# Sliding-window attention block on one core: score sets of five chunks cut into 32x64 tiles, 50 sets for 60

## The chip, the cores and the metric

The kernel runs on one core of one Trainium2 chip. The metric is device time in microseconds (us) of one launch; less is better. A core has five engines with an instruction queue each: PE (TensorE, matrix products; PEld are its weight loads), ACT (ScalarE), DVE (VectorE), POOL (GpSimd) and SP (here only DMA issues).

## The reference, cut to what matters

x has 2048 rows of 640. The block is a modulated LayerNorm, windowed attention with 32 heads of 20, a gated sum, a second LayerNorm and a gated MLP (1536 wide):

```python
qkv = (x @ wqkv).reshape(B, S, 3, 32, 20)          # h of LayerNorm 1 stands for x
scores = einsum('bhqd,bhkd->bhqk', q, k) * 20 ** -0.5
mask = (idx[:, None] - idx[None, :] >= 0) & (idx[:, None] - idx[None, :] < 256)
p = softmax(where(mask, scores, -1e9))
x = x + ga * (einsum('bhqk,bhkd->bhqd', p, v) @ wo)
x = x + gb * ((sigmoid(h2 @ w_gate) * (h2 @ w_up)) @ w_down)   # h2: LayerNorm 2 of x
```

A query sees itself and the 255 positions before it.

## The kernel before

The 2048 rows are eight chunks (0 to 7) of 256 queries, two blocks of 128 each. For a chunk and four key blocks (two blocks back, one back, and the chunk's own two: -2, -1, 0, 1) the heads go in two groups q of 16; a group is four k, and each k is four heads j that stand in the four 32-row strips of PE (20 of the 32 rows are used).

- **Scores.** One score set fills the single buffer S, four PSUM banks (bank j for strip j) of 512 columns: keys lie on the 128 partitions, queries along the columns. A matmul for strip j is `tp=(32*j, 0)`, a 32x128 tile: four heads at a time. From chunk 1 on a group has six sets: for each k one with key blocks 0 and -1 against both query blocks (8 matmuls of 256 columns), and for each pair of k one with the two edge products, block -2 against query block 0 and block 1 against query block 1 (16 matmuls of 128).
- **Exp and masks.** ACT takes exp of the whole set (128x2048) into one of eight buffers E; no maximum is taken off. POOL then sets the dead part of the triangular blocks to zero with affine_select (L983 and L985): 512 elements each per partition in the main sets, 1024 in the edge sets.
- **Weighted sum.** `burst` is the product with V for a group: 64 matmuls of 256 or 128 columns in 128x32 tiles, `tp=(0, 32*j)`, four heads at a time in four column strips. It waits for all masks of its group. With `AFTER = 1` it stands ahead of the second score set of the next group, in the same planned step (`both_of`).
- **The rest of PE's work**: q, k, v projections, output projection (wo), MLP (wg, wu, wd), all in full 128x128 tiles and recorded on L625; tiled matmuls are L626.
- **Order.** Every operation has a place in a hand-out table: `PLAN` is a list of numbers (operation times 5 plus engine) that a planner made offline, and `SLOTS` the buffer that each tile takes. Each engine issues in that order and waits by semaphore.
- **Q and K transposed.** From chunk 1 on, DMA transposes on SP's queue turn the staged q and k into QT and KT (QT is [block, head group, query]).

Of the kernel before, what the change touches and what calls it, by code (L numbers as in the profile page):

```python
# [305 lines left out]
def c_pe(n):  # L306
# [119 lines left out]
PQ = ()  # L426
KEEP = 3
DSAFE = 1.0
NPB = 0
OUTE = ("sp", "act")  # L430
XE = ("sp", "act")
MW = 64
WM1 = (3, 5)
QM = ()
AFTER = 1
NOW = 1
LEAD = 2
HEAT = (5, 1, 1, 1)
# [8 lines left out]
def build(nc, A_x, A_wqkv, A_wo, B_x, B_w_gate, B_w_up, B_w_down, c, w_mod, out, S=2048):  # L447
# [480 lines left out]

    last = {"s": heat}

    def plan(a):


        if a == 0:
# [115 lines left out]
    def attention(a):  # L1050
# [8 lines left out]
        for q in range(2):  # L1059
            sets = plan(a)  # L1060
            Es = []
            for si, (ps, md, mf) in enumerate(sets):
                now = pend.pop(0) if pend and si == AFTER else None
                Es.append(score_set(a, q, si, ps, md, mf, now[0]() if now else None))
                if now:
                    now[1]()
# [175 lines left out]
```

## Time and profile before

| | |
|---|---|
| time of 3 runs | median 329.04 us (327.99 to 329.66) |
| profiled execution, first to last instruction (span) | 327.1 us |
| median less that span | 1.9 us |
| PE busy | 318.7 us, 97% |
| ACT busy | 231.4 us, 71% |
| DVE busy | 196.7 us, 60% |
| POOL busy | 183.0 us, 56% |
| granted TensorE clock | 1.000 |

The profile is of one execution; of its time only the span is recorded. Busy time of PE counts overlapping matmul records once. In lists of groups each row is a line, an engine, an operation and its tiles, with the count behind x, the busy time and the mean length of one record in ns, and then the idle time just ahead of them with what ended it. A matmul record lasts from its start to its modelled end, so records overlap; what a matmul takes of PE is the distance to the next start. In the timeline, rows are start, length, engine, line, operation, tiles, count.

### The profile page before, as it was taken

The page shows a single profiled execution, that of the slowest core. Times are in us where ns is not written, and L with a number is a line of the kernel's source. Part 1 is how long each engine was busy: PE and PEld are TensorE (multiplying, and loading weights), DVE is VectorE, ACT ScalarE, POOL GpSimd, SP SyncE. Part 2 cuts the span into 40 slices and gives each one's busy share as a digit, 9 for nine tenths or more (in the row PEclk, how much of TensorE's full clock was granted, in tenths as well). Part 3 has the DMA queues.
Part 4 walks back from the last instruction along what each step waited for, and adds up shares of the span by engine and source line. Part 5 has one row for each costly group of instructions (what it writes and reads, how often), then busy time and mean ns, then how long its engine had stood idle before and what let it go on. Part 6 is the DMA issues. An engine that isn't in the chain of part 4 may idle for free.

```text
span 327.1 us, 9812 instructions
## 1 busy us (share of the span) xinstructions
PE 318.7 (97%) x4123; PEld 227.8 (70%) x4123; DVE 196.7 (60%) x422; ACT 231.4 (71%) x227; POOL 183.0 (56%) x279
## 2 busy tenths in 40 slices
PE   5999899999999999999999999999999999999997
PEld 2666556567776777665767667766777777788885
DVE  6796799678485545675457554456727463484333
ACT  2489799987787898879797968785897568322120
POOL 4248579789688563778383745646490837402000
DMA  7989899999902281321802100360051012202101
GB/s 231 373 319 196 178 271 192 222 289 274 218 18 40 42 139 34 82 42 44 170 0 44 32 2 19 80 125 2 1 82 42 2 42 43 82 0 42 40 2 40
DMA packets 64613, 33.52 MB, mean 102 GB/s; under 512 B 49082, under 2 KB 63034, under 8 KB 64570
## 3 DMA queue, kind: packets, MB, share of 16 engines
q1 hardware_dynamic: 63200, 31.27, 42.2%
q10 hardware_dynamic: 1370, 1.64, 1.5%
q8 instruction: 32, 0.52, 0.7%
q14 instruction: 11, 0.09, 0.1%
HBM read 18.35 MB, written 2.62 MB: 64 GB/s over the span
## 4 chain that ended last, share of the span: by engine, by line
PE 93%; DMA 3%; DVE 1%; ACT 1%; issue 0%; POOL 0%; SPq 0%; DVEq 0%
PE M L625 77%; PE S L626 9%; PE M L626 7%; DMA QT<-stg 1%; DMA x<-in_A_x_dram 1%; ACT E L975 1%; DVE st L732 1%; DVE x L753 0%; SPq L524 0%; POOL st L740 0%; ACT QT L655 0%; DVE hT L814 0%; DVE st L734 0%; DVE x L1159 0%; POOL st L738 0%
## 5 line engine op out<-in xcount | busy, mean ns | idle before, releaser
L975 ACT ACTIVATE E<-S 128x2048 bf16<-128x2048 f32 x90 | 169.0, 1877 | 36.3 <-PE S L626 34.4
L983 POOL TENSOR_SCALAR_AFFINE_SELECT E<-E 128x512 bf16<-128x512 bf16 (+2 forms) x90 | 73.7, 830 | 36.2 <-ACT E L975 15.1
L985 POOL TENSOR_SCALAR_AFFINE_SELECT E<-E 128x512 bf16<-128x512 bf16 (+1 forms) x84 | 65.6, 790 | 36.4 <-ACT E L975 30.7
L625 PE MATMUL M<-h2T,wu 128*128 128x256 bf16 x480 | 73.6, 273 | 0.0
L625 PE MATMUL M<-h2T,wg 128*128 128x256 bf16 x480 | 72.7, 273 | 0.0
L1140 DVE SCALAR_TENSOR_TENSOR hh<-sig,M 128x512 bf16<-128x512 f32 x48 | 32.4, 681 | 49.5 <-ACT sig L1138 27.2
L625 PE MATMUL M<-wd,hh 128*128 128x320 bf16 (+2 forms) x396 | 60.5, 295 | 0.0
L625 PEld LDWEIGHTS M<-h2T,wu 128*128 128x128 bf16 x480 | 45.1, 98 | 10.8 <-issue 2.7
L1138 ACT ACTIVATE sig<-M 128x512 f32<-128x512 f32 x48 | 28.5, 596 | 33.5 <-PE M L625 32.4
L625 PEld LDWEIGHTS M<-h2T,wg 128*128 128x128 bf16 x480 | 45.2, 98 | 9.9 <-issue 1.9
L625 PEld LDWEIGHTS M<-wd,hh 128*128 128x128 bf16 x396 | 36.8, 98 | 14.9 <-issue 1.9
L626 PE MATMUL S<-QT,KT 20*128 20x256 bf16 (+1 forms) x960 | 35.9, 245 | 1.8 <-DMA QT<-stg 1.3
L626 PEld LDWEIGHTS S<-QT,KT 20*128 20x128 bf16 x960 | 14.1, 92 | 21.9 <-ACT E L975 11.6
L732 DVE BATCH_NORM_STATS2 st<-x 128x6 f32<-128x320 bf16 x64 | 29.0, 476 | 0.6 <-DMA x<-in_A_x_dram 0.5
L625 PE MATMUL M<-wk,hT 128*128 128x320 bf16 x160 | 29.4, 300 | 0.0
L1021 DVE STREAM_TRANSPOSE T<-M 128x512 f32<-128x512 f32 x32 | 21.6, 698 | 12.7 <-PE S L626 12.2
L625 PE MATMUL M<-wv,hT 128*128 128x320 bf16 x160 | 28.6, 300 | 0.0
L625 PE MATMUL M<-wo,oT 128*128 128x320 bf16 x160 | 28.0, 300 | 0.0
L625 PE MATMUL M<-wq,hT 128*128 128x320 bf16 x160 | 27.6, 300 | 0.3 <-DVE hT L814 0.3
L1159 DVE TENSOR_TENSOR x<-M,x 128x320 bf16<-128x320 f32 (+2 forms) x33 | 15.4, 475 | 17.9 <-PE M L625 17.6
L1094 DVE TENSOR_TENSOR x<-M,x 128x320 bf16<-128x320 f32 x32 | 15.3, 486 | 16.0 <-PE M L625 15.3
L656 DVE CAST stg<-M 128x320 bf16<-128x320 f32 x33 | 15.7, 483 | 12.5 <-PE M L625 12.4
(82 smaller groups left out, 303.2 us busy)
## 6 DMA issues: line engine op xcount, KB each, us to landing
x<-in_A_x_dram SPq DMA_DIRECT2D x10, 320.0 KB, 4.3
wd<-in_w_mod_dram SPq DMA_DIRECT2D x6, 320.0 KB, 5.1
wd<-in_B_w_down_dram SPq DMA_DIRECT2D x4, 480.0 KB, 5.0
out_dram<-x SPq DMA_DIRECT2D x4, 320.0 KB, 2.4
wg<-in_B_w_gate_dram SPq DMA_DIRECT2D x2, 576.0 KB, 7.3
wu<-in_B_w_up_dram SPq DMA_DIRECT2D x2, 576.0 KB, 5.9
wu<-in_w_mod_dram SPq DMA_DIRECT2D x1, 960.0 KB, 11.0
out_dram<-x ACTq DMA_DIRECT2D x3, 320.0 KB, 2.3
```

The source lines that it names most:

```text
L625: return e.matmul(o, l, r, start=st, stop=sp, skip_group_check=True)
L626: return e.matmul(o, l, r, start=st, stop=sp, tile_position=tp, skip_group_check=True)
L656: return e.tensor_copy(dst(), src())
L732: A("dve", lambda e, g, bi=bi, j=j: e.bn_stats(v(bi * 12 + j * 6, 6), src[bi].ap[:, j * 320:(j + 1) * 320]), 0.48, reads=[src[bi].r()], wr ...
L975: A("act", lambda e, eng: e.activation(E.ap[:], Sp.ap[:], ACT.Exp, scale=SM_SCALE), 1.876, reads=[Sp.r()], writes=[E.r()], prio=3, tag=f"e ...
L983: return e.affine_select(ap, ap, pattern=[[0, ap.shape[1]], [1, 128]], compare_op=ALU.is_ge, fill=0.0, base=0, channel_multiplier=-1)
L985: return e.affine_select(ap, ap, pattern=[[0, ap.shape[1]], [-1, 128]], compare_op=ALU.is_ge, fill=0.0, base=-1, channel_multiplier=1)
L1021: A("dve", lambda e, g, h=h: e.transpose(T1.ap[:, 512 * h:512 * h + 512], X[h].ap), 0.694, reads=[X[h].r()], writes=[T1.r(h)], prio=3.5, t ...
L1094: A("dve", lambda e, g, ps=ps, bi=bi, half=half: e.tensor_tensor(x1[bi].ap[:, half * 320:half * 320 + 320], ps.ap[:, 0:320], x1[bi].ap[:, ...
L1138: A("act", lambda e, g, pg=pg, sg=sg: e.activation(sg.ap[:], pg.ap[:], ACT.Tanh, scale=0.5), c_act(512), reads=[pg.r()], writes=[sg.r()], ...
L1140: A("dve", lambda e, g, pu=pu, sg=sg, f0=f0: e.scalar_tensor_tensor(out=hh.ap[:, f0:f0 + 2, :], in0=sg.ap[:].rearrange("p (a b) -> p a b", ...
L1159: A("dve", lambda e, g, ps=ps, bi=bi, c0=c0, n=n: e.tensor_tensor(x1[bi].ap[:, c0:c0 + n], ps.ap[:, 0:n], x1[bi].ap[:, c0:c0 + n], op=ALU. ...
```

## The change

Chunks 3 to 7 get five score sets a group instead of six, ten groups in all (chunks 1 and 2, named in `WHOLE`, and chunk 0 keep theirs). The triangular blocks have a dead 64x64 quarter each. Within a main set of one k, the dead quarter of block 0 (keys 64 to 127, queries 0 to 63) is not computed and its place takes the live quarter of block -2 (keys 64 to 127, queries 64 to 127); the dead quarter of block -1 takes the live quarter of block 1 (keys 0 to 63, queries 128 to 191). Lower and upper 64 keys thus see different columns, so a main set is 24 matmuls in 32x64 tiles, `tp=(32*j, 0)` and `tp=(32*j, 64)`, of 64, 192 and 256 columns. What is left of the edge products, for all four k, is one edge set: 32 matmuls of 64 columns in 32x128 tiles. It is the third of the five sets (`ESI = 2`).

The edge set's exp goes out to a tile that spans two neighbouring E buffers, with room for the two corner quarters of each k; `spread` copies these from the main set with affine_select (256 elements), which also zeroes the rest. So a group still holds six buffers.

```diff
+NE = 8
+ESI = 2
+WHOLE = (1, 2)
-    p_QT = sbpool("QT", 3, [128, 2, NG, 128])
+    p_QT = sbpool("QT", 3, [128, NG, 2, 128])
...
+    def edge_set(a, q, si):
+        F, F2 = Tile(p_E, f"F{a}_{q}"), Tile(p_E, f"G{a}_{q}")
+        F.mate, F2.mate = F2, F
...
+        for k in range(4):
+            prods += [(k, -2, 0, 128, 0, 64, 128 * k), (k, 1, 0, 128, 192, 64, 128 * k + 64)]
...
+        mask(a, 1024, select(lambda: cols(0), lambda: cols(0), [[0, 16], [-1, 64]], -1, 1), [F.r()], [F.r(-2)], (F2,))
+        mask(a, 1024, select(lambda: cols(192), lambda: cols(192), [[0, 16], [1, 64]], 64, -1), [F.r()], [F.r(1)], (F2,))
...
+    def main_set(a, q, k, si):
+        E = Tile(p_E, f"E{a}_{q}_{k}")
+        prods = [(k, 1, 0, 64, 128, 64, 192), (k, -2, 64, 64, 64, 64, 256), (k, -1, 0, 64, 0, 192, 0), (k, 0, 64, 64, 64, 192, 320),
+                 (k, 0, 0, 64, 0, 256, 256), (k, -1, 64, 64, 0, 256, 0)]
...
+    def spread(a, q, k, E, F, fa):
+        mask(a, 256, select(lambda: fa()[:, :, k, 128:192], lambda: E.ap[:, :, 192:256], [[0, 4], [1, 64]], 0, -1),
+             [E.r()], [F.r((k, 1)), E.r("s1")], (F.mate,))
+        mask(a, 256, select(lambda: fa()[:, :, k, 64:128], lambda: E.ap[:, :, 256:320], [[0, 4], [-1, 64]], -65, 1),
+             [E.r()], [F.r((k, -2)), E.r("s2")], (F.mate,))
+        mask(a, 512, ...)   # block -1's triangle, after s1
+        mask(a, 512, ...)   # block 0's triangle, after s2
```

A product is (k, key block, first key, keys, first query, queries, column in S). QT's new layout puts a head group's 256 queries side by side; chunk 0's copies and the DMA transposes of the later chunks write into it with a stride. `PLAN` is new from its 721st place on, and `SLOTS` with it; the first 720 places, into chunk 2, are the old ones.

How the last three sets of a group (chunk 7, second group) stand on PE. Before, two main sets and the second edge set, with MLP matmuls between:

```order
L626 MATMUL S<-QT,KT 128x256 x8
L625 MATMUL M<-wd,hh 128x320 x16
L626 MATMUL S<-QT,KT 128x256 x8
L625 MATMUL M<-wd,hh 128x320 x16
L626 MATMUL S<-QT,KT 128x128 x16
L625 MATMUL M<-wd,hh 128x320 x12
```

After, the last three sets of the same group:

```order
L635 MATMUL S<-QT,KT 128x64 x32
L634 MATMUL M<-wd,hh 128x320 x16
L635 MATMUL S<-QT,KT 64x64 x8
L635 MATMUL S<-QT,KT 64x192 x8
L635 MATMUL S<-QT,KT 64x256 x8
L634 MATMUL M<-wd,hh 128x320 x20
L635 MATMUL S<-QT,KT 64x64 x8
L635 MATMUL S<-QT,KT 64x192 x8
L635 MATMUL S<-QT,KT 64x256 x8
```

A main set is now three rows of eight, and the edge set comes once, ahead of the last two main sets.

The second place is the product with V of chunk 7's first group. On PE after the change, from that group's last main set (first three rows) on:

```order
L635 MATMUL S<-QT,KT 64x64 x8
L635 MATMUL S<-QT,KT 64x192 x8
L635 MATMUL S<-QT,KT 64x256 x8
L634 MATMUL M<-h2T,wg 128x256 x8
L634 MATMUL M<-h2T,wu 128x256 x6
L634 MATMUL M<-wo,oT 128x320 x3
L634 MATMUL M<-h2T,wu 128x256 x4
L634 MATMUL M<-wo,oT 128x320 x5
L634 MATMUL M<-h2T,wg 128x256 x4
L634 MATMUL M<-wo,oT 128x320 x5
L634 MATMUL M<-h2T,wg 128x256 x2
L634 MATMUL M<-h2T,wu 128x256 x2
```

and right behind it the next group's first main set, more filler, and the product with V (rows with E,V):

```order
L635 MATMUL S<-QT,KT 64x64 x8
L635 MATMUL S<-QT,KT 64x192 x8
L635 MATMUL S<-QT,KT 64x256 x8
L634 MATMUL M<-h2T,wu 128x256 x2
L634 MATMUL M<-wo,oT 128x320 x5
L634 MATMUL M<-h2T,wu 128x256 x4
L634 MATMUL M<-h2T,wg 128x256 x4
L634 MATMUL M<-h2T,wu 128x256 x12
L635 MATMUL M<-E,V 32x256 x32
L635 MATMUL M<-E,V 32x128 x32
```

On POOL, before the change, the last masks that this product waits for are those of 8x128, of the group's edge sets:

```order
L985 AFFINE_SELECT E<-E 128x4x128 x2
L983 AFFINE_SELECT E<-E 128x4x128
L985 AFFINE_SELECT E<-E 128x4x128
L983 AFFINE_SELECT E<-E 128x4x128
L983 AFFINE_SELECT E<-E 128x8x128
L985 AFFINE_SELECT E<-E 128x8x128 x2
L738 TENSOR_SCALAR st<-st 128x2
```

After it, the first row here is the first mask that waits for the exp of the group's last main set, and the product waits for all of them down to the last 4x128:

```order
L947 AFFINE_SELECT E<-E 128x4x64 x3
L947 AFFINE_SELECT E<-E 128x4x128
L947 AFFINE_SELECT E<-E 128x4x64
L947 AFFINE_SELECT E<-E 128x4x128 x2
L947 AFFINE_SELECT E<-E 128x4x64
L947 AFFINE_SELECT E<-E 128x4x128 x3
L747 TENSOR_SCALAR st<-st 128x2
```

Eleven short masks, of several k, stand there now instead of edge masks of 1024.

More of the change, by code (lines that the diff above doesn't have):

```diff
@@ L432 @@
 MW = 64
+NE = 8
+ESI = 2
+WHOLE = (1, 2)
 WM1 = (3, 5)
-QM = ()
 AFTER = 1
@@ L902, in qkv @@
             for key, dst in (("q", QT[a]), ("k", KT[a])):
-                for b0, b1 in ((0, 2),) if a in QM else ((0, 1), (1, 2)):
-                    rs = [(bi, half) for bi in range(b0, b1) for half in range(2)]
-                    transp_dma(lambda dst=dst, b0=b0, b1=b1: dst.ap[:, b0:b1].rearrange("p b t c -> p (b t) c"),
-                               lambda s=stg[key], b0=b0, b1=b1: s.ap[:, b0:b1].rearrange("p b d -> p (b d)"), 3, 0.87 * (b1 - b0),
-                               [stg[key].r(k) for k in rs], [dst.r(k) for k in rs], 1.25 if b1 - b0 == 1 else 2.0, f"qkt{a}")
+                for bi in range(2):
+                    rs = [(bi, half) for half in range(2)]
+                    transp_dma(lambda key=key, dst=dst, bi=bi: turned_heads(key, dst, bi),
+                               lambda s=stg[key], bi=bi: s.ap[:, bi, :], 3, 0.87,
+                               [stg[key].r(k) for k in rs], [dst.r(k) for k in rs], 1.25, f"qkt{a}")
         for bi in range(2):
@@ L945, in score_set, with queries, select @@
-    def score_set(a, q, si, ps, md, mf, before):
-        E, Sp = Tile(p_E, f"E{a}_{q}_{si}"), Tile(p_S, f"S{a}_{q}_{si}")
+    def queries(a, gi, c0, n):
+        return lambda j: QT[a].ap[32 * j:32 * j + DH, gi, :, :].rearrange("p b c -> p (b c)")[:, c0:c0 + n]
+    def select(dst, src, pattern, base, mul):
+        return lambda e, eng: e.affine_select(dst(), src(), pattern=pattern, compare_op=ALU.is_ge, fill=0.0, base=base, channel_multiplier=mul)
+    def score_set(a, q, si, tag, prods, low, E, dst, src, more=()):
+        Sp = Tile(p_S, f"S{a}_{q}_{si}")
@@ L956, in sc @@
             return ins
         rd = {}
-        for k, kb, u, n, cu in ps:
-            kc = (2 * a + kb) // 2
-            rd[KT[kc].r((kb % 2, q))] = 1
+        for _, kb, _, _, _, _, _ in prods:
+            rd[KT[(2 * a + kb) // 2].r((kb % 2, q))] = 1
             for bi in range(2):
                 rd[QT[a].r((bi, q))] = 1
-        if before is None:
-            last["s"] = [A("pe", sc, 0.213 + 0.03, reads=list(rd), writes=[Sp.r()], prio=10, lat=0.2, tag=f"score{a}",
-                           extra=last["s"], mode=1, hold=[E])]
+        md = 3 if low else 1
@@ L966, in score_set @@
+        now = pend.pop(0) if pend and si == AFTER else None
+        if now is None:
+            last["s"] = [A("pe", sc, 0.243, reads=list(rd), writes=[Sp.r()], prio=10, lat=0.2, tag=f"{tag}{a}",
+                           extra=last["s"], mode=md, hold=[E, *more])]
         else:
-            pa, pv, pd, prd, X = before
+            pa, pv, pd, prd, X, hold = now[0]()
             def both_of(e, eng):
@@ L973, in score_set @@
             last["s"] = [A("pe", both_of, pd + 0.09 + 0.243, reads=list(rd), writes=[Sp.r(), X[0].r(), X[1].r()], prio=10, lat=0.2,
-                           tag=f"pvs{pa}", extra=last["s"], mode=2, mout=1, hold=[E] + X)]
-        A("act", lambda e, eng: e.activation(E.ap[:], Sp.ap[:], ACT.Exp, scale=SM_SCALE), 1.876,
-          reads=[Sp.r()], writes=[E.r()], prio=3, tag=f"exp{a}")
-        out_r = [E.r()]
-        for kind, lst in ((0, md), (1, mf)):
-            for c0, stride, n in lst:
-                def mk(e, eng, kind=kind, c0=c0, stride=stride):
-                    ap = E.ap[:].rearrange("p j (t c) -> p (j t) c", c=128 * stride)[:, :, 128 * c0:128 * c0 + 128]
-                    if kind == 0:
-                        return e.affine_select(ap, ap, pattern=[[0, ap.shape[1]], [1, 128]], compare_op=ALU.is_ge, fill=0.0,
-                                               base=0, channel_multiplier=-1)
-                    return e.affine_select(ap, ap, pattern=[[0, ap.shape[1]], [-1, 128]], compare_op=ALU.is_ge, fill=0.0,
-                                           base=-1, channel_multiplier=1)
-                nel = 4 * (4 // stride) * 128
-                A("pool", mk, c_pool(nel), reads=[E.r()], writes=[E.r((kind, c0))], prio=5, tag=f"mask{a}")
-                out_r.append(E.r((kind, c0)))
@@ L990, in score_set, with mask @@
-        return E, out_r
-    def burst(a, q, sets, Es):
+                           tag=f"pvs{pa}", extra=last["s"], mode=2, mout=md, hold=[E, *more, *hold, *X])]
+        A("act", lambda e, eng: e.activation(dst(), src(Sp.ap), ACT.Exp, scale=SM_SCALE), 1.876,
+          reads=[Sp.r()], writes=[E.r()], prio=3, tag=f"exp{a}", hold=more)
+        if now is not None:
+            now[1]()
+    def mask(a, n, fn, reads, writes, hold=()):
+        A("pool", fn, c_pool(n), reads=reads, writes=writes, prio=5, tag=f"mask{a}", hold=hold)
@@ new lines, in first_sets @@
+    def first_sets(q):
+        a, out = 0, []
+        for si, (ps, w) in enumerate(([((0, 0, 0, 2, 0), (1, 0, 0, 2, 2)), 2], [((2, 0, 0, 2, 0), (3, 0, 0, 2, 2)), 2],
+                                      [tuple((k, 1, 1, 1, k) for k in range(4)), 4])):
+            E = Tile(p_E, f"E{a}_{q}_{si}")
+            score_set(a, q, si, "score", [(k, kb, 0, 128, 128 * u, 128 * n, 128 * at) for k, kb, u, n, at in ps], False, E,
+                      lambda E=E: E.ap[:], lambda s: s[:])
+            st = 1 if w == 4 else 2
+            ap = lambda E=E, st=st: E.ap[:].rearrange("p j (t c) -> p (j t) c", c=128 * st)[:, :, 0:128]
+            mask(a, 16 // st * 128, select(ap, ap, [[0, 16 // st], [1, 128]], 0, -1), [E.r()], [E.r("m")])
+            for k, kb, u, n, at in ps:
+                out.append((k, kb, u, n, lambda j, E=E, at=at, n=n: E.ap[:, j, 128 * at:128 * (at + n)], [E.r(), E.r("m")]))
+        return out
@@ new lines, in whole_sets @@
+    def whole_sets(a, q):
+        out, si = [], 0
+        for p in range(2):
+            halves = [([(k, 0, 0, 2, 0), (k, -1, 0, 2, 2)], ((0, 0, 4),), ((1, 3, 4),)) for k in (2 * p, 2 * p + 1)]
+            halves.append(([(2 * p, -2, 0, 1, 0), (2 * p, 1, 1, 1, 1), (2 * p + 1, -2, 0, 1, 2), (2 * p + 1, 1, 1, 1, 3)],
+                           ((0, 1, 2),), ((1, 0, 2),)))
+            for ps, md, mf in halves:
+                E = Tile(p_E, f"E{a}_{q}_{si}")
+                score_set(a, q, si, "score", [(k, kb, 0, 128, 128 * u, 128 * n, 128 * at) for k, kb, u, n, at in ps], False, E,
+                          lambda E=E: E.ap[:], lambda s: s[:])
+                rs = [E.r()]
+                for kind, c0, st in md + mf:
+                    ap = lambda E=E, st=st, c0=c0: E.ap[:].rearrange("p j (t c) -> p (j t) c", c=128 * st)[:, :, 128 * c0:128 * c0 + 128]
+                    mask(a, 16 // st * 128, select(ap, ap, [[0, 16 // st], [1 - 2 * kind, 128]], -kind, 2 * kind - 1), [E.r()], [E.r((kind, c0))])
+                    rs.append(E.r((kind, c0)))
+                for k, kb, u, n, at in ps:
+                    out.append((k, kb, u, n, lambda j, E=E, at=at, n=n: E.ap[:, j, 128 * at:128 * (at + n)], rs))
+                si += 1
+        return out
@@ new lines, in sets @@
+    def sets(a, q):
+        if a == 0:
+            return first_sets(q)
+        if a in WHOLE:
+            return whole_sets(a, q)
+        F, fa, Es = None, None, []
+        for si in range(5):
+            if si == ESI:
+                F, fa = edge_set(a, q, si)
+                done = range(len(Es))
+            else:
+                Es.append(main_set(a, q, len(Es), si))
+                done = [len(Es) - 1] if F is not None else []
+            for k in done:
+                spread(a, q, k, Es[k], F, fa)
+        out = []
+        for k, E in enumerate(Es):
+            rs = [E.r(), E.r("d"), E.r("g")]
+            out.append((k, -1, 0, 2, lambda j, E=E: E.ap[:, j, 0:256], rs))
+            out.append((k, 0, 0, 2, lambda j, E=E: E.ap[:, j, 256:512], rs))
+        for k in range(4):
+            out.append((k, -2, 0, 1, lambda j, k=k: fa()[:, j, k, 0:128], [F.r(), F.r(-2), F.r((k, -2))]))
+            out.append((k, 1, 1, 1, lambda j, k=k: fa()[:, j, k, 128:256], [F.r(), F.r(1), F.r((k, 1))]))
+        return out
@@ L994, in burst @@
+    def burst(a, q, pieces):
         X = [Tile(p_M, f"O{a}_{q}x"), Tile(p_M, f"O{a}_{q}y")]
@@ L999, in pv @@
             seen = set()
-            for (E, _), st in zip(Es, sets):
-                for k, kb, u, n, cu in st[0]:
-                    bank = k // 2
-                    oc = (k % 2) * 256 + u * 128
-                    for j in range(4):
-                        h = NG * j + 4 * q + k
-                        ins = mm(e, X[bank].ap[32 * j:32 * j + 32, oc:oc + n * 128], V[2 * a + kb].ap[:, h * VW:h * VW + 32],
-                                 E.ap[:, j, cu * 128:(cu + n) * 128], (bank, j) not in seen, True, tp=(0, 32 * j))
-                        seen.add((bank, j))
+            for k, kb, u, n, ap, _ in pieces:
+                bank = k // 2
+                oc = (k % 2) * 256 + u * 128
+                for j in range(4):
+                    h = NG * j + 4 * q + k
+                    ins = mm(e, X[bank].ap[32 * j:32 * j + 32, oc:oc + n * 128], V[2 * a + kb].ap[:, h * VW:h * VW + 32],
+                             ap(j), (bank, j) not in seen, True, tp=(0, 32 * j))
+                    seen.add((bank, j))
             return ins
         rd = {}
-        for E, rs in Es:
+        for _, _, _, _, _, rs in pieces:
             rd.update(dict.fromkeys(rs))
@@ L1015, in burst @@
             rd[V[2 * a + kb].r(1)] = 1
-        return a, pv, len(sets) * 512 / 2400.0 * 1.04 + 0.02, rd, X
+        hold = list(dict.fromkeys(r.tile.mate for r in rd if r.tile is not None and r.tile.mate is not None))
+        return a, pv, sum(n for _, _, _, n, _, _ in pieces) * 128 / 2400.0 * 1.04 + 0.02, rd, X, hold
     def norm(X, Tn, oT, a, q):
@@ L1035, in build, with later @@
     pend = []
-    def later(a, q, sets, Es, close):
+    def later(a, q, pieces, close):
         made = []
         def first():
-            made.append(burst(a, q, sets, Es))
+            made.append(burst(a, q, pieces))
             return made[0]
@@ L1045, in alone @@
     def alone(first, then):
-        pa, pv, pd, prd, X = first()
-        A("pe", pv, pd, reads=list(prd), writes=[X[0].r(), X[1].r()], prio=8, lat=0.2, tag=f"pvs{pa}", mode=2, hold=X, extra=last["s"])
+        pa, pv, pd, prd, X, hold = first()
+        A("pe", pv, pd, reads=list(prd), writes=[X[0].r(), X[1].r()], prio=8, lat=0.2, tag=f"pvs{pa}", mode=2, hold=hold + X, extra=last["s"])
         then()
@@ L1059, in attention @@
         for q in range(2):
[L1060 to L1066, printed above, removed]
+            pieces = sets(a, q)
             if a < NOW:
-                alone(*later(a, q, sets, Es, close))
+                alone(*later(a, q, pieces, close))
             else:
-                pend.append(later(a, q, sets, Es, close))
+                pend.append(later(a, q, pieces, close))
     def add_pair(x, pss, prio, tag):
```

52 lines of the change are left out of this document (28 added, 24 removed), and 211 rows, old and new, of the table PLAN.

## The prediction

> **What bounds the kernel now.** I read the page first, then the busy time by stage, the chain of work that ended last, and the timeline of PE. From the page, and from the stages (length, then busy time and count of PE, PEld, DVE, ACT and POOL, the granted clock, DMA):
>
> ```profile
> span 327.1 us, 9812 instructions
> PE 318.7 (97%) x4123; PEld 227.8 (70%) x4123; DVE 196.7 (60%) x422; ACT 231.4 (71%) x227; POOL 183.0 (56%) x279
> PE M L625 77%; PE S L626 9%; PE M L626 7%; DMA QT<-stg 1%; DMA x<-in_A_x_dram 1%; ACT E L975 1%; DVE st L732 1%; DVE x L753 0%; SPq L524 0%; POOL st L740 0%; ACT QT L655 0%; DVE hT L814 0%; DVE st L734 0%; DVE x L1159 0%; POOL st L738 0%
> 116.00:285.00 169.00, 168.98 (x2315) 121.78 (x2313) 90.78 (x178) 131.54 (x113) 100.65 (x142) 1.00 0.26 52
> 285.00:327.00 42.00, 39.78 (x356) 32.72 (x344) 19.99 (x38) 7.67 (x13) 2.57 (x5) 1.00 0.10 27
> ```
>
> The chain is PE for 93% of the span, and in the stage that the change rewrites (116 to 285 us, roughly chunks 3 to 7) PE is busy 168.98 of 169 us. So time is PE's time: what leaves PE there leaves the span, as long as no new wait opens, and ACT (131.5 of 169) and POOL (100.7) matter only through waits. Behind the last product with V the chain (start, length, what) is filler alone:
>
> ```profile
> 265.27 1.43 PE M L626 x64
> 266.70 0.33 PE S L626 x8
> ...
> 283.71 1.43 PE M L626 x64
> 285.14 39.65 PE M L625 x344
> ```
>
> An earlier end of attention therefore moves this block of 39.65 us forward as a whole.
>
> **What a score set costs PE.** From the timeline of PE, a main set, an edge set, two runs of plain matmuls, a product with V, and a run of 64-column matmuls:
>
> ```profile
> 180.38 0.38 PE L625 MATMUL M<-h2T,wu 128*128 128x256 bf16 x2
> 180.69 0.40 PE L626 MATMUL S<-QT,KT 20*128 20x256 bf16 x8
> 181.03 0.45 PE L625 MATMUL M<-wk,hT 128*128 128x320 bf16 x2
> ...
> 185.16 0.71 PE L625 MATMUL M<-wd,hh 128*128 128x320 bf16 x4
> 185.79 0.40 PE L626 MATMUL S<-QT,KT 20*128 20x128 bf16 x16
> 186.13 0.85 PE L625 MATMUL M<-wo,oT 128*128 128x320 bf16 x5
> ...
> 187.23 0.84 PE L625 MATMUL M<-wq,hT 128*128 128x320 bf16 x5
> 187.91 0.84 PE L625 MATMUL M<-wv,hT 128*128 128x320 bf16 x5
> ...
> 191.69 1.50 PE L626 MATMUL M<-E,V 128*32 128x256 bf16 x64
> 193.13 0.40 PE L626 MATMUL S<-QT,KT 20*128 20x256 bf16 x8
> ...
> 10.04 0.46 PE L625 MATMUL S<-silubc,wd 128*128 128x64 bf16 x10
> 10.33 0.38 PE L612 MATMUL S<-E 128*128 128x512 bf16 x1
> ```
>
> Five matmuls of 320 columns take 187.91 - 187.23 = 0.68 us, 0.136 each, or 2.35 columns per ns; 256 columns are 0.109 us. The two ahead of the main set end their share at 180.38 + 0.22 = 180.60, and plain work goes on at 181.03: the set costs 0.43 us. The edge set: 185.16 + 4 x 0.136 = 185.70, to 186.13, again 0.43. In both, 512 columns in four strips at once are 0.22 us (512 / 2350), and 0.21 goes into changing over to small tiles and back.
>
> **Taken away.** In chunks 3 to 7, 60 sets x 0.43 = 25.8 us. The products with V keep their 64 matmuls, and all other matmuls stay.
>
> **Put in: 40 main sets of 24 matmuls.** Lower and upper keys are 512 columns each. If the two halves run at once, all eight tiles side by side, the columns take 0.22 us as before; if they run in turn, 0.44. No row has row and column tiles together. Column tiles alone do run at once: the product with V puts 64 matmuls of 192 columns on average into 193.13 - 191.69 - 0.1 (change of tiles) = 1.34 us, 9,200 columns per us, 3.9 times the single rate. Row strips alone too: 8 x 256 columns in 0.22 us are the same 3.9 times. The ends are thus 0.43 and 0.65 us a set. I take 0.46, near the low end, since both kinds of neighbour run nearly fourfold; the 0.03 are for the second half's four matmuls, which start behind the first's, and for weights that are due after 64 columns instead of 128. 40 x 0.46 = 18.4 us (ends 17.2 and 26.0).
>
> **Put in: 10 edge sets of 32 matmuls.** Full-height matmuls of 64 columns come every 0.029 us (10.33 - 10.04 over 10) for 64 / 2350 = 0.027; eight fours of them add 8 x 0.002 to 0.43, so 0.45. Were instructions the limit, at the 14 ns apiece of the 16-matmul set (0.22 / 16), 32 would take 0.45 instead of 0.22, or 0.66 a set. The 14 ns are no such limit, being just 128 columns in four strips, so I take 0.45: 4.5 us (ends 4.3 and 6.6).
>
> **PE's sum**: 18.4 + 4.5 - 25.8 = -2.9 us; at the low ends -4.3, at the high ends +6.8.
>
> **ACT, POOL and the waits.** Groups of ACT and POOL, and of weight loads:
>
> ```profile
> L975 ACT ACTIVATE E<-S 128x2048 bf16<-128x2048 f32 x90 | 169.0, 1877 | 36.3 <-PE S L626 34.4 <-POOL E L985 0.7
> L985 POOL TENSOR_SCALAR_AFFINE_SELECT E<-E 128x512 bf16<-128x512 bf16 x56 | 35.5, 640 | 29.2 <-ACT E L975 24.1 <-DVE x L753 2.5 <-DVE Tn L1025 2.5
> L983 POOL TENSOR_SCALAR_AFFINE_SELECT E<-E 128x1024 bf16<-128x1024 bf16 x32 | 34.9, 1092 | 18.6 <-ACT E L975 11.4 <-DVE oT L1032 4.2 <-ACT V L655 2.1
> L983 POOL TENSOR_SCALAR_AFFINE_SELECT E<-E 128x2048 bf16<-128x2048 bf16 x2 | 4.0, 2004 | 0.5 <-ACT E L975 0.5
> L626 PEld LDWEIGHTS M<-E,V 128*32 128x32 bf16 x960 | 19.9, 97 | 4.1 <-issue 2.3 <-POOL E L983 1.2 <-POOL E L985 0.3
> L626 PEld LDWEIGHTS S<-QT,KT 20*128 20x128 bf16 x960 | 14.1, 92 | 21.9 <-ACT E L975 11.6 <-issue 8.0 <-DVE KT L656 0.5
> ```
>
> ACT loses 10 x 1.877 = 18.8 us in that stage; it waits for PE there, so this buys nothing by itself. Exp's length with the edge set's strided output has no row; all 90 have 2048 elements and none is late, so even 0.2 us more on 10 of them is hidden.
>
> POOL: a group had 8 x 0.640 + 4 x 1.092 = 9.5 us of masks. A quarter mask of 256 elements has no row; by the slope from 512 to 1024 it is 0.640 - 0.226 = 0.41 us, and if its four runs set the price instead of the elements, 0.64. By elements a group becomes 2 x 1.092 + 8 x 0.41 + 8 x 0.640 = 10.6 us, +11 us in all on an engine that has 68 us to spare in the stage. The margin is what matters: the product with V waits for its last mask, as it does now for short times (1.2 and 0.3 us in total in the first row of weight loads). At the place of chunk 7's first group shown above, exp starts some 0.45 us behind the set's first load and lasts 1.88, as in these two rows:
>
> ```profile
> 193.13 0.12 PEld L626 LDWEIGHTS S<-QT,KT 20*128 20x128 bf16 x8
> 193.58 1.88 ACT L975 ACTIVATE E<-S 128x2048 bf16<-128x2048 f32 x1 [1.54 <-PE S L626]
> ```
>
> Five quarter masks and six of 512 then are 5 x 0.41 + 6 x 0.640 = 5.9 us, so the last ends 8.2 us after the set's start. PE meanwhile has the set (0.34 to the next plain matmul), 26 matmuls of 256 and 13 of 320 columns (4.6), a main set with its changes (0.46), 22 and 5 more (3.1), and a change of tiles (0.1): 8.6 us. It is met with 0.4 us in hand, less the wake-ups between engines. Nothing is queued behind a waiting product but the score set of the same step and PE's later work, so a delay goes into the span in full. For ten such places I put in 0.4 us together (ends 0 and 8, each product 0.8 us late if quarter masks cost 0.64 at this place: 5 x 0.23 - 0.4).
>
> Costed at nothing: QT's new layout. It keeps 128 columns of a block together, and the same DMA transposes are issued. It has one exposed place: the chain has a transfer of 4.59 us ahead of chunk 1's first score set.
>
> ```profile
> 30.37 4.59 DMA QT<-stg
> 35.05 0.40 PE S L626 x8
> ```
>
> If writing with a stride were slower, by 10% say, 0.5 us would show there at once. The tail is covered: h2T of chunk 7 is ready at 303.0, 17.9 us after the last product with V ended at 285.14,
>
> ```profile
> 301.39 1.63 POOL L769 TENSOR_SCALAR h2T<-h2T,scB,shB 128x256 bf16<-128x256 bf16 x3 [4.92 <-DMA h2T<-x]
> ```
>
> and the plain work placed between the two on PE goes from 96 matmuls of 256 and 64 of 320 columns (19.2 us) to 28 and 116 (18.8).
>
> **Sum**: -2.9 + 0.4 = -2.5 us. The profiled span of 327.1 becomes 324.6; the median of the runs shown lies 1.9 us above the span and moves along, 329.04 - 2.5 = 326.5 us.
>
> **Rivals.**
>
> *No change, weights late (0.17).* A load's record is 92 to 97 ns long, and in a main set the second product's weights are due 27 ns after the first's, not 54 or 109. If the rest, 97 - 27 = 0.07 us, shows once a set, 40 x 0.07 = 2.8 us eat the gain: 329.3 us. Against it: in the product with V four new tiles start every 84 ns on average (1.34 us / 16) without waiting out 97 ns. The Trainium skill speaks against the change here: "TensorEngine Tiling (Array Packing)", section "Tile-to-Partition Mapping", says column tiling turns fast weight load off, and "TensorE: Matmul & The Clock Gate", section "LDWEIGHTS", gives columns / 1.2 ns. By these, as an estimate, 64 columns load in 53 ns, the two halves of a strip in 107 ns if in turn, some 0.2 us more a main set and 8 us in all, about 334 us. By that rule the four loads of 32 columns ahead of each four of the product with V would be 107 ns in turn, and the 84 ns measured say that loads of different tiles overlap.
>
> *Slower, halves in turn (0.11).* Both halves of a strip read different queries from the same 20 partitions, and no row shows that one strip can stream two columns at once. Then main sets cost 0.65: 40 x 0.65 + 4.5 - 25.8 + 0.4 = +4.9, 333.9 us. It decides from 0.52 us a main set on, (25.8 - 4.5 - 0.4) / 40.
>
> *POOL releases late (0.09).* If masks cost by runs, edge masks of 16 runs take the 2.0 us of the 2048 row and quarter masks 0.64; a group has 14.2 us of masks, and products wait about 1 us each: 326.1 + 10 = 336 us. Half of that, with small wake-ups on POOL's own waits, gives 331. Against it: the three mask rows fit elements and runs alike, so nothing but the average load (100 of 169 us) speaks.
>
> That fewer sets do not come about is excluded by PE's order.
>
> **Chances.** Forecast 0.60 (its own range 324.9 to 327.4), weights late 0.17, halves in turn 0.11, POOL late 0.09, a slower transfer or tail 0.03. Two medians of this kernel differ by up to 0.5% (1.6 us; the three runs span 1.7) without meaning. Faster than 327.4: the forecast and a part of the milder cases, 0.64. Within 327.4 to 330.7: 0.21. Slower: 0.15. The range leaves out the upper rivals at 334 and above: 324.6 to 330.9.
>
> **What would show it.** Right: PE goes from a main set's start to the next plain matmul in about 0.37 us; the three product forms of 64 rows of output show starts close together in eights; the stage stays without idle PE; the last product with V ends 2 to 4 us earlier; about 39 us of plain matmuls follow. Wrong: 0.56 or more from a main set to the next matmul (halves in turn), 0.41 to 0.5 (weights), weight loads of E,V waiting for POOL by more than 1 us in sum over the ten groups, quarter masks at 0.64, or a longer QT transfer at 30 us.

## The result and the profile after

| | before | after |
|---|---|---|
| median of 6 runs each, on one chip | 329.22 us (327.99 to 329.90) | 326.19 us (324.54 to 327.52) |
| ratio of the two, 95% interval | | 0.9915 (0.9886 to 0.9945) |
| profiled execution | span 327.1 | 327.33 us, span 325.6 |

The change saves 3.0 us, 0.9%; the forecast was 2.5, to 326.5 us. The page of after (span, busy time, shares of the chain), and its two stages with the columns as before:

```profile
span 325.6 us, 11132 instructions
PE 317.3 (97%) x4762; PEld 231.7 (71%) x4763; DVE 198.7 (61%) x424; ACT 214.5 (66%) x220; POOL 194.5 (60%) x334
PE 89%; POOL 3%; ACT 3%; DMA 3%; DVE 1%; issue 1%; SPq 0%; ACTq 0%; DVEq 0%; POOLq 0%
116.00:285.00 169.00, 168.95 (x2933) 127.94 (x2932) 94.60 (x184) 118.45 (x110) 113.52 (x199) 1.00 0.24 47
285.00:327.00 42.00, 38.32 (x323) 30.73 (x321) 19.99 (x40) 5.77 (x10) 1.50 (x3) 1.00 0.14 40
```

In the stage that was rewritten PE is as full as before (168.95 of 169 us); ACT fell by 13 us there (ten exps less, 18.8 us, but seven other instructions more in this stretch), POOL rose by 13, and neither took PE's place. PE's share of the chain is 89% instead of 93% because the chain turns off to ACT and POOL between 92.3 and 108.3 us, ahead of chunk 2's last product with V, which waits 0.35 us for its masks. The spans differ by 1.5 us only, because this execution began its score sets later. The rows of the score products' matmuls on PE, of before and then of after, give the start of the first and of the last (18.9 and 20.3 us for the first):

```profile
L626 PE MATMUL S<-QT,KT x960: 211/244/279, 18.9 to 278.6; 20*128 20x256 bf16 x96, 20*128 20x128 bf16 x96
```

```profile
L635 PE MATMUL S<-QT,KT x1600: 188/234/278, 20.3 to 272.9; 20*64 20x256 bf16 x36, 20*128 20x64 bf16 x36, 20*64 20x64 bf16 x35, 20*64 20x192 bf16 x35
```

The chain of after ends so (start, length, what):

```profile
273.17 10.15 PE M L634 x92
283.32 1.43 PE M L635 x64
284.75 38.58 PE M L634 x324
```

From the first score set to the end of the filler it is 284.75 + 38.58 - 20.3 = 303.0 us, and before 285.14 + 39.65 - 18.9 = 305.9: 2.9 us less. That agrees with the runs. The order of all other work from chunk 2 on is new too, and the matmul records tell the two apart. From the first score set's start to the last matmul's start after is 2.87 us shorter than before: the score sets with the changes of tiles around them give -3.0, the gaps ahead of the products with V +0.47, and the gaps between plain matmuls -0.31, while the columns of the plain matmuls are the same 239.7 us. (A gap is the distance between two starts less the first one's columns at 2.35 per ns.) So the new score sets made the gain; the new order and the new masks together cost 0.2 us. The 1.4 us at the start come and go, since the first score set of the kernels profiled here began anywhere from 18.9 to 20.8 us.

The timeline of PE in after, an edge set (32 matmuls) and two main sets (24; a row merges their forms and names the first):

```profile
265.21 1.79 PE L634 MATMUL M<-wd,hh 128*128 128x320 bf16 x12
266.94 0.41 PE L635 MATMUL S<-QT,KT 20*128 20x64 bf16 x32
267.28 2.35 PE L634 MATMUL M<-wd,hh 128*128 128x320 bf16 x16
269.56 0.43 PE L635 MATMUL S<-QT,KT 20*64 20x64 bf16 x24
269.92 0.31 PE L634 MATMUL M<-wd,hh 128*128 128x320 bf16 x1
...
198.89 0.57 PE L634 MATMUL M<-wd,hh 128*128 128x320 bf16 x3
199.39 0.43 PE L635 MATMUL S<-QT,KT 20*64 20x64 bf16 x24
199.75 0.50 PE L634 MATMUL M<-h2T,wg 128*128 128x256 bf16 x3
```

From the set's first matmul to the next plain one a main set takes 0.36 us (269.56 to 269.92; 199.39 to 199.75) and an edge set 0.34. The change of tiles ahead of a set is the rest: the twelve matmuls at 265.21 end their share at 265.21 + 12 x 0.136 = 266.84, and the set starts at 266.94, 0.10 later.

### The profile page after: what moved, and what is told of

Its sections match the earlier page's. It is cut to its first block, busy times and chain, and to the rows that moved or that the text cites. A ratio compares the mean times of both kernels' runs of the same rounds, so it can differ in the third digit from the quotient of the medians.

```text
span 325.6 us, 11132 instructions
## 1 busy us (share of the span) xinstructions
PE 317.3 (97%) x4762; PEld 231.7 (71%) x4763; DVE 198.7 (61%) x424; ACT 214.5 (66%) x220; POOL 194.5 (60%) x334
## 4 chain that ended last, share of the span: by engine, by line
PE 89%; POOL 3%; ACT 3%; DMA 3%; DVE 1%; issue 1%; SPq 0%; ACTq 0%; DVEq 0%; POOLq 0%
PE M L634 73%; PE S L635 8%; PE M L635 7%; POOL E L947 3%; ACT E L981 2%; DMA QT<-stg 1%; DMA x<-in_A_x_dram 1%; PE S L634 1%; PE S L621 1%; DVE x L762 0%; SPq L533 0%; POOL st L749 0%; ACT QT L664 0%; DVE hT L823 0%; DVE st L741 0%
## 5 line engine op out<-in xcount | busy, mean ns | idle before, releaser
L947 POOL TENSOR_SCALAR_AFFINE_SELECT E<-E 128x256 bf16<-128x256 bf16 (+2 forms) x234 | 149.8, 671 | 53.2 <-ACT E L981 34.6
L981 ACT ACTIVATE E<-S 128x2048 bf16<-128x2048 f32 x80 | 150.2, 1877 | 43.8 <-PE S L635 43.2
L634 PE MATMUL M<-h2T,wu 128*128 128x256 bf16 x480 | 66.4, 273 | 0.0
L634 PE MATMUL M<-h2T,wg 128*128 128x256 bf16 x480 | 65.8, 273 | 0.0
L634 PE MATMUL M<-wd,hh 128*128 128x320 bf16 (+2 forms) x396 | 56.4, 295 | 0.0
L635 PE MATMUL S<-QT,KT 20*64 20x64 bf16 (+5 forms) x1600 | 33.3, 231 | 1.8 <-DMA QT<-stg 1.3
L635 PEld LDWEIGHTS S<-QT,KT 20*64 20x64 bf16 (+1 forms) x1600 | 15.2, 99 | 19.7 <-ACT E L981 9.8
L634 PE MATMUL M<-wq,hT 128*128 128x320 bf16 x160 | 26.0, 300 | 0.2 <-DVE hT L823 0.2
L747 POOL TENSOR_SCALAR st<-st 128x2 f32<-128x2 f32 (+1 forms) x17 | 4.0, 233 | 32.4 <-DVE st L743 31.5
L635 PEld LDWEIGHTS M<-E,V 128*32 128x32 bf16 x960 | 19.9, 97 | 4.6 <-issue 2.4
## 6 DMA issues: line engine op xcount, KB each, us to landing
wu<-in_w_mod_dram SPq DMA_DIRECT2D x1, 960.0 KB, 10.3
```

The costliest lines, as they stand in the source:

```text
L634: return e.matmul(o, l, r, start=st, stop=sp, skip_group_check=True)
L635: return e.matmul(o, l, r, start=st, stop=sp, tile_position=tp, skip_group_check=True)
L747: A("pool", lambda e, g, lo=lo, w=w: e.tensor_scalar(v(28 + lo, w), var()[:, lo:lo + w], EPS, None, op0=ALU.add), 0.2, reads=[st.r(("m", b ...
L947: return lambda e, eng: e.affine_select(dst(), src(), pattern=pattern, compare_op=ALU.is_ge, fill=0.0, base=base, channel_multiplier=mul)
L981: A("act", lambda e, eng: e.activation(dst(), src(Sp.ap), ACT.Exp, scale=SM_SCALE), 1.876, reads=[Sp.r()], writes=[E.r()], prio=3, tag=f"e ...
```

## The experiments

The two theories at the start. **Mine**: all eight 32x64 tiles run at once, a main set costs what an old one cost plus a few hundredths, and PE's sum over sets is the whole effect; ACT and POOL do not count. **The rival**: the gain is relief of ACT (ten exps less) or is set by the release through POOL, and two halves run at once only because the code pairs them. All kernels are edits of after, but for the short exp. "Set" is the median distance from a main set's first matmul to the next plain matmul behind the whole set; "marks" the distance from the first score matmul's start to the last matmul's start in the profiled execution (305.7 us before, 302.8 after). Ratios are to the kernel before on the same chip.

| kernel | median us (runs) | ratio, 95% | set us | marks us |
|---|---|---|---|---|
| after | 326.19 (6) | 0.9915 (0.9886 to 0.9945) | 0.362 | 302.8 |
| halves apart | 326.90 (10) | 0.9921 (0.9892 to 0.9950) | 0.388 | 302.4 |
| full height | 325.18 (4) | 0.9875 (0.9833 to 0.9918) | 0.330 | 301.8 |
| two passes | 337.46 (4) | 1.0249 (1.0207 to 1.0292) | 0.604 | 313.8 |
| changeover | 337.00 (4) | 1.0236 (1.0184 to 1.0289) | 0.630 | 311.7 |
| short exp (on before) | 329.64 (12) | 1.0011 (0.9985 to 1.0036) | | |
| tiny quarters | 325.99 (7) | 0.9900 (0.9864 to 0.9936) | | |
| long first | 326.01 (6) | 0.9900 (0.9856 to 0.9944) | 0.359 | |
| strips apart | 328.94 (1; before 331.03) | 0.994, one run | 0.402 | 304.5 |
| two apart | 342.94 (1; before 331.03) | 1.036, one run | 0.763 | 319.3 |

**Halves apart.** The three products of the lower keys first, then the three of the upper.

```diff
-        prods = [lower 64, upper 64, lower 192, upper 192, lower 256, upper 256]
+        prods = [lower 64, lower 192, lower 256, upper 64, upper 192, upper 256]
```

> The changed kernel, but each main set of chunks 3 to 7 issues its three lower products first and then its three upper ones. Theory (PE starts matmuls in order, and the halves overlap only because the code alternates them): the upper half starts about when the lower half's last product of 256 columns does, 0.11 us late, so 40 x 0.11 = +4.3 us against the changed kernel's 326.2: 330.5 us, and a main set takes about 0.47 us from its start to the next plain matmul instead of 0.36. Rival 1 (the halves are independent queues, order does not matter): 326.2. Rival 2 (halves never overlap, or the strip is blocked by its other half): 0.22 a set, 335 us.

The timeline of PE, one set with its neighbours:

```profile
151.10 0.57 PE L634 MATMUL M<-wd,hh 128*128 128x320 bf16 x3
151.60 0.46 PE L635 MATMUL S<-QT,KT 20*64 20x64 bf16 x24
151.99 0.58 PE L634 MATMUL M<-wv,hT 128*128 128x320 bf16 x3
```

The set grew by 0.026 us (151.60 to 151.99), not by a tenth. The theory that matmuls start in the order of the code, on which the larger figure stood, fell. Median starts of the single matmul records of a set, the first of each four, in ns from the set's start:

```
after, as in the code   L64 0   U64 13  L192 52  U192 66  L256 138  U256 152  next plain 362
halves apart            L64 0   U64 40  L192 53  U192 93  L256 138  U256 178  next plain 388
```

With the halves apart the code has L64, L192, L256 ahead of U64, yet U64 starts 13 ns before L192. Of the 26 ns all is the upper half's later start; 40 sets make 1.0 us. The marks are 0.4 us shorter than in after, though: after's execution waited 1.3 us for chunk 1's QT (first row below, from the waits of PE in after: total, times, longest), the one with halves apart has no such row.

```profile
PE S L635 <- DMA QT<-stg: 1.3, 1, 1.3
PE M L635 <- POOL E L947: 0.3, 1, 0.3
```

The gap ahead of that set is 1.41 us by the records; put back, the marks are +1.0. That wait comes and goes between executions; none of the edits touches what runs before chunk 3.

**Full height.** The main set in two products of 32x128 tiles.

```diff
+        prods = [(k, 0, 0, 128, 0, 256, 256), (k, -1, 0, 128, 0, 256, 0)]
```

> The changed kernel, but the 40 main sets are computed as before, 8 matmuls of 256 columns in 32x128 tiles; the live corner quarters are left out, so part of the edge scores is missing. All orders and all other work stay. Theory (a main set in small tiles costs 0.03 us more than one of full height): 40 x 0.03 = -1.2 us, 325.0 us. Rival (the small tiles cost much more, and something else gave the gain): 322 or less. Rival (PE's price of a set does not matter, ACT's relief made the gain): 326.2.

```profile
267.23 0.40 PE L635 MATMUL S<-QT,KT 20*128 20x256 bf16 x8
267.56 2.21 PE L634 MATMUL M<-wd,hh 128*128 128x320 bf16 x15
```

In the timeline of PE the set is back at 0.33. The marks fell by 1.0, and 40 x 0.032 = 1.3 were due; this execution has a wait of 0.3 us near the start that after has not. This is the price of cutting a main set into halves: 1.0 to 1.3 us in all.

**Two passes.** Every product of a main set twice, the first pass and then the same again.

```diff
+        prods = prods + prods
```

> The changed kernel, with all 24 matmuls of each main set of chunks 3 to 7 issued twice (same results). Theory (PE is the bound, its time goes into the span in full): 40 x 0.23 = +9 us, 335.2 us. Rival (ACT or POOL bound these chunks and PE has slack): under +3 us, 329 or less.

```profile
151.90 0.67 PE L635 MATMUL S<-QT,KT 20*64 20x64 bf16 x48
152.50 0.45 PE L634 MATMUL M<-wd,hh 128*128 128x320 bf16 x2
```

The second pass adds 0.242 us (0.604 - 0.362). It is 512 columns in each of eight tiles, 4096 in all; one after another they would take 4096 / 2350 = 1.74 us, so 7.2 tiles ran at once on average. The marks grew by 11.0 us, the sets by 40 x 0.242 = 9.7. The other 1.3 is one wait of PE for DVE (1.3 us) that after doesn't have: behind the set at 144.4 us the next plain matmul comes after 2.00 us instead of 0.60.

**Changeover.** One full-size 64-column matmul put between the first and the second pair of a main set, into columns that the set overwrites.

```diff
+                if low and kb == -2:
+                    mm(e, Sp.ap[:, 0, 0:64], ident[:], ident[:, 0:64], True, True)
```

> The changed kernel, with one plain 128x128 matmul of 64 columns put into each main set of chunks 3 to 7 behind its first two products (its output in S is overwritten by a later product of the set): two more changes of tiles a set. Theory (a change out of and into small tiles costs 0.2 us a pair, so that ten sets fewer saved 2 us in changes alone): 40 x (0.21 + 0.03 for the columns) = +9.6 us, 335.8 us. Rival (the change is hidden behind loads or neighbours and only the columns count): 40 x 0.03 = +1.1 us, 327.3 us.

```profile
203.92 0.24 PE L635 MATMUL S<-QT,KT 20*64 20x64 bf16 x8
204.09 0.20 PE L634 MATMUL S<-ident 128*128 128x64 bf16 x1
204.22 0.40 PE L635 MATMUL S<-QT,KT 20*64 20x192 bf16 x16
204.55 1.27 PE L634 MATMUL M<-h2T,wg 128*128 128x256 bf16 x10
```

The set goes from 0.362 to 0.630 (203.92 to 204.55): one matmul worth 0.027 us costs 0.268, so 0.24 are the two changes of tiles, with the second start in small tiles; 0.21 was expected. For the old sets the same price is 0.426 (distance and gap ahead) - 0.218 (512 columns) = 0.21, and this is what each of ten fewer sets saves beside its columns. The marks (+8.9, or +10.3 with after's QT wait put back, which this execution too didn't have) are near 40 x 0.268 = 10.7; the gaps ahead of the products with V are 0.4 us shorter here.

**Short exp.** On the kernel before: in chunks 3 to 7 the exp of the 20 edge sets over half the columns.

```diff
+        nj = 2 if a >= 3 and si in (2, 5) else 4
+        A("act", lambda e, eng: e.activation(E.ap[:, 0:nj], Sp.ap[:, 0:nj], ...
```

> The kernel before, with the exp of the 20 edge sets of chunks 3 to 7 over half the set (1024 elements instead of 2048; the other half of the buffer keeps old values, so part of the weights is wrong): ACT gets 20 x 0.94 = 18.8 us less to do, as in the change, and PE the same. Theory (the gain is PE's): 329.2 us, no change within 0.5. Rival (ACT's relief made the gain): about 326.2 us.

The stage row and the group of short exps:

```profile
116.00:285.00 169.00, 168.98 (x2268) 121.37 (x2270) 90.54 (x180) 117.46 (x114) 100.71 (x142) 1.00 0.25 51
L976 ACT ACTIVATE E<-S 128x1024 bf16<-128x1024 f32 x20 | 20.5, 1023 | 7.1 <-PE S L626 6.8
```

ACT got as much relief as in after (117.46 of 169 us, after 118.45), and the ratio is 1.0011 (0.9985 to 1.0036). Relief of ACT bought nothing; this rival is out.

**Tiny quarters.** The quarter masks over 8 columns instead of 64.

```diff
-             ... fa()[:, :, k, 128:192], E.ap[:, :, 192:256], [[0, 4], [1, 64]] ...
+             ... fa()[:, :, k, 128:136], E.ap[:, :, 192:200], [[0, 4], [1, 8]] ...
```

> The changed kernel, with the 80 quarter masks over 8 columns instead of 64 (32 elements instead of 256; 7/8 of the corner quarters is not copied, so part of the weights is stale). POOL gets about 80 x 0.2 = 16 us less. Theory (POOL is late for the products with V by 0.5 us in all): -0.5 us, 325.7 us, and the excess waits ahead of the products with V go. Rival (POOL bounds part of these chunks): -3 us or more, 323 us.

The mask group and the weight loads of the product with V:

```profile
L947 POOL TENSOR_SCALAR_AFFINE_SELECT E<-E 128x32 bf16<-128x32 bf16 x80 | 18.7, 246 | 32.3 <-ACT E L981 24.6 <-DVE x L762 3.0 <-DVE h2T L778 2.5
L635 PEld LDWEIGHTS M<-E,V 128*32 128x32 bf16 x960 | 19.9, 97 | 4.5 <-issue 2.5 <-POOL E L947 1.6 <-POOL st L747 0.2
```

A quarter mask fell from 427 to 246 ns, the wait for POOL from 1.7 to 1.6 us, and the ratio cannot be told from after's. My expectation that the waits ahead of the products would go with the shorter masks was wrong: above the plain change of tiles, the gaps ahead of the ten products sum to 0.26 us in both kernels. POOL's quarter masks are not a cost worth chasing here.

**Long first.** The pairs of a main set in the order 256, 192, 64, to see whether the 25 ns that the first pair takes above its columns (52 - 27) belong to its 64 columns or to its place.

```diff
+        prods = [lower 256, upper 256, lower 192, upper 192, lower 64, upper 64]
```

> The changed kernel with the products of a main set in falling order, 256, 192 and 64 columns instead of 64, 192, 256. In the changed kernel the first pair of 64 columns takes 0.052 us to the second pair's start instead of the 0.027 of its columns. Theory (the second pair's weights are not yet loaded after 27 ns): behind 256 columns they are, and the set shrinks by about 0.02 us, 40 x 0.02 = -0.8 us, 325.4 us. Rival (it is the fill behind the change of tiles, whatever comes first): no change, 326.2 us.

```profile
151.78 0.43 PE L635 MATMUL S<-QT,KT 20*64 20x256 bf16 x24
152.13 0.45 PE L634 MATMUL M<-wv,hT 128*128 128x320 bf16 x2
```

By the records the second pair now starts 133 ns after the first, 24 above the 109 of 256 columns: the extra time goes with the place behind the change of tiles, not with short products, and the theory of weights not loaded after 27 ns fell with it. The order of the pairs is worth next to nothing (0.359 for 0.362).

**Strips apart and two apart.** What decides when a tile starts? Strips apart writes all six products of strip 0, then those of strip 1, and so on. Two apart writes the lower half's products twice, then the upper half's twice.

```diff
+            for ... in [(*p, j) for j in range(4) for p in prods]     # strips apart
+        prods = lower * 2 + upper * 2                                 # two apart
```

> The changed kernel, but each main set of chunks 3 to 7 issues strip after strip: the six matmuls of head strip 0, then those of strip 1, 2 and 3. After the first experiment (halves apart cost 0.026 us a set and not 0.11) two readings stand. Reading 1 (each tile of PE starts its matmuls as soon as its own are next, whatever stands ahead in the code for other tiles; only issue is in order, about 3.4 ns for a weight load and its matmul): strip 3 starts 18 x 3.4 = 61 ns late, and a set takes about 0.36 + 0.05 = 0.41 us from its start to the next plain matmul, +2 us in all. Reading 2 (matmuls start in program order, and the two halves were a special case of two neighbours): each strip starts when the last products of the strip before it start, 0.11 us apart at least, 0.36 + 3 x 0.11 = 0.7 us a set or more, +13 us.

> Every main set of chunks 3 to 7 computed twice, as in the run with two passes (0.604 us from a set's start to the next plain matmul there), but with both passes of the three lower products ahead of both passes of the three upper ones. Reading 1 (tiles start on their own, issue costs 3.4 ns a pair): the upper half starts 24 x 3.4 = 82 ns late, 0.604 + 0.07 = 0.67 us. Reading 2 (program order): the upper half starts with the last lower product, some 0.35 us late, 0.95 us a set.

Timelines of PE, strips apart first:

```profile
200.22 0.47 PE L635 MATMUL S<-QT,KT 20*64 20x64 bf16 x24
200.63 1.26 PE L634 MATMUL M<-h2T,wg 128*128 128x256 bf16 x10
```

```profile
151.43 0.83 PE L635 MATMUL S<-QT,KT 20*64 20x64 bf16 x48
152.19 2.35 PE L634 MATMUL M<-wd,hh 128*128 128x320 bf16 x16
```

Single records, first of each four or two, ns from the set's start:

```
strips apart   64s of strips 0, 1, 2, 3 at 0, 20, 40, 60;  first 192s at 52, 72, 93, 113;  next plain 402
two apart      64s at 0, first 192s at 53, first 256s at 138;  the second half's 64s at 154;  next plain 763
```

Strips apart: strip 3 starts at 60 ns although 18 matmuls of 64 to 256 columns stand ahead of it in the code: 60 / 18 = 3.3 ns for each, the same 3.3 that separate neighbours in the records and that put U64 at 40 ns behind 12 matmuls above. It looks as if PE goes past a matmul whose tile is busy, at 3.3 ns each; the records show the starts, not the reason. Two apart shows the bound: 24 matmuls stand ahead of the upper half, which by that would start at 80 ns; it started at 154, just behind the lower half's third products (138). At that moment 12 of the 24 had started and 12 were pending, three in each strip. Whether the limit is 12 in all or three for a strip, and whether it counts matmuls or their weight loads, these kernels don't tell. Neither of the two readings expected for two apart gave 0.763; the measurement lies between them. The marks bear both sets out: +1.7 us for 40 x 0.040, and +16.5 for 40 x 0.401 (one wait for DVE of 1.0 us is in it).

No kernel here that does the whole work beats after by more than can be measured: long first lies on it. Tiny quarters and full height leave parts of the work out, and only full height is faster, in its sets and its marks.

## Why the prediction was right

- **Main sets, the step with the wide range.** Put in at 0.46 us each between 0.43 and 0.65; measured 0.362 plus 0.0935 for the change into small tiles (median of the gaps, worked out as above), 0.455. The eight tiles run at once (two passes: 0.242 us more for another 1024 columns in every strip, which in turn would be 0.44). The 0.03 that I added for halves and weights is confirmed in size: against full height, the last pair starts 18 ns later (138 for 120), and eight starts spread over 24 ns where four spread over 10; 32 ns together.
- **Edge sets.** Put in at 0.45; measured 0.345 + 0.096 = 0.441.
- **Sum on PE.** By the same records the old sets took 40 x 0.425 + 20 x 0.431 = 25.6 us, the new 40 x 0.455 + 10 x 0.441 = 22.6: -3.0 against -2.9 forecast. The whole forecast of -2.5 was 0.4 short of the 2.87 counted above; 0.3 of that are the gaps between plain matmuls, which the prediction did not count and whose cause stays open. Ten sets fewer save 10 x 0.425 = 4.25 us, about half of it changes of tiles (10 x 0.21) and half columns (10 x 0.218); the halves give back 40 x 0.030 = 1.2.
- **Waits for POOL.** I put in 0.4 us over ten places. The groups of after:

```profile
L981 ACT ACTIVATE E<-S 128x2048 bf16<-128x2048 f32 x80 | 150.2, 1877 | 43.8 <-PE S L635 43.2
L947 POOL TENSOR_SCALAR_AFFINE_SELECT E<-E 128x512 bf16<-128x512 bf16 x112 | 70.5, 648 | 10.2 <-DVE wo L1272 3.5 <-ACT E L981 1.2 <-DVE x L762 1.0
L947 POOL TENSOR_SCALAR_AFFINE_SELECT E<-E 128x1024 bf16<-128x1024 bf16 x40 | 45.7, 1156 | 17.1 <-ACT E L981 13.6 <-ACT V L664 2.0 <-DVE wd L1206 0.8
L947 POOL TENSOR_SCALAR_AFFINE_SELECT E<-E 128x256 bf16<-128x256 bf16 x80 | 33.1, 427 | 25.4 <-ACT E L981 19.3 <-DVE x L762 2.2 <-DVE h2T L778 1.9
L635 PEld LDWEIGHTS M<-E,V 128*32 128x32 bf16 x960 | 19.9, 97 | 4.6 <-issue 2.4 <-POOL E L947 1.7 <-POOL h2T L778 0.3
```

  Exp with the strided output of edge sets costs the same 1.877 us. A quarter mask costs 427 ns, near the 414 by elements and far from 0.64; of the 40 masks of 1024, 20 are the old form and 20 the new one of 16 runs, about 2 x 1156 - 1092 = 1220 ns in the mean (18 of these 20 took 1142 to 1149, two 1722 and 1959). Weight loads of the product with V wait 1.7 us for POOL in all, 1.5 before; in the ten new groups 0.4 us, 0.8 before, so the sign of more than 1 us did not show. In these groups the gaps above the plain change of tiles sum to 0.26 us, 0.15 before: the change brought 0.1 us there, not 0.4. One place I had not named makes up the rest: chunk 2's last product, whose sets are the old ones, now waits 0.35 us for its masks (start, length, what, from the chain):

```profile
103.77 4.50 POOL E L947 x6
108.31 1.50 PE M L635 x64
```

  With tiny quarters it waits 0.32: it isn't the new masks' work but where the order puts the old ones. So the term of 0.4 us came out in size (0.47 over all products with V) by luck, three quarters of it at a place that the prediction did not have.
- **QT's layout at nothing.** The transfer ahead of chunk 1's first set took 4.59 us, and in the chain of after

```profile
31.74 4.66 DMA QT<-stg
```

  it takes 0.07 more, below what that spot varies by.
- **The tail, covered, but wrong in its form.** I looked for a last product with V 2 to 4 us earlier and 39 us of filler behind it. Against the first score set it came 1.8 us earlier (284.75 - 20.3 against 285.14 - 18.9), and the filler shrank by 1.1 us (39.65 to 38.58; 324 matmuls for 344): the order moved some of it ahead of the product. The sum is the same 2.9.
- **Rivals.** Weights late would have shown 0.41 to 0.5 for 0.362. The Trainium skill's rule beside it ("TensorE: Matmul & The Clock Gate", section "LDWEIGHTS"; by the estimate in the prediction about 334 us if the loads of a strip's two halves came in turn) did not show: with twice the loads, 0.024 us a set appear at the first pair, and 0.011 in the full-height set. Halves in turn is out by two passes, POOL late by the row of loads and the 427 ns of a quarter mask.

## To carry to other kernels

Where small tiles stand between full-size matmuls, count the entries first: a pair of changes cost 0.21 to 0.24 us here, as much as all the columns of a set, so merging sets pays even when it needs more and smaller matmuls. Fill a dead quarter with live work of another product by splitting a tile in two, since row and column tiles run side by side (7.2 of 8). Then look at whether the engine relieved was ever waited for: as much relief of ACT as ten exps gave was worth nothing by itself.

## What the hardware showed beyond this

- Matmuls of different tiles start out of the order of the code. With the halves apart U64 starts 13 ns ahead of L192 that the code has before it, and with strips apart strip 3 starts at 60 ns, when 10 of the 18 matmuls ahead of it in the code have not started. The Trainium skill, "TensorE: Matmul & The Clock Gate", section "Packing small matmuls — row/col tiling", says that matmuls keep the order of the program in start and end; here the starts of different tiles don't. Ends are modelled in these records and prove nothing. The same skill's "TensorEngine Tiling (Array Packing)", section "Key Properties", says that different tiles can load and multiply in parallel, and that agrees with 0.242 us for eight times 512 columns.
- The look-ahead has an end: with 24 matmuls ahead, the second half started at 154 ns, not at 80.
- Order inside a set costs little up to 12 or 18 matmuls written ahead (0.388 and 0.402 for 0.362 us) and much at 24 (0.763 for 0.604, both with 48 matmuls).
- The first products behind a change of tiles take 24 to 25 ns above their columns in 32x64 tiles (64 or 256 columns) and 11 to 12 ns in 32x128 ones (64, 128 or 256).
